# A Mamba-2 scan in front of expert routing: decays along rows of `a`, y's halves by sequences, states summed in PSUM

## Chip, cores and metric

One core of one Trainium2 chip runs the kernel. The metric is device time in microseconds (us). Times are medians over repeated executions; the profile is one execution of its own.

## What is computed

The first block is a Mamba-2 scan over 4 sequences b, 8 heads h, 768 positions, head width D = 32 and state width N = 16. The second sends each of the 3072 tokens (256 channels, all heads of one position) through one of 8 experts, chosen by a hash of its token id.

```python
log_a = np.log(np.clip(a, 1e-06, 1.0))
for c in range(nc):                                # chunks of positions
    cum = np.cumsum(la, axis=-1)
    L = np.exp(cum[:, :, :, None] - cum[:, :, None, :]) * causal
    y_intra = np.einsum('bhij,bhjd->bhid', np.einsum('bhin,bhjn->bhij', Cc, Bc) * L, xc)
    y_inter = np.einsum('bhin,bhnd->bhid', Cc, state) * np.exp(cum)[:, :, :, None]
    y[:, :, sl] = y_intra + y_inter
    decay_from_j = np.exp(cum[:, :, -1:] - cum)
    Bx = np.einsum('bhjn,bhjd->bhjnd', Bc, xc) * decay_from_j[:, :, :, None, None]
    state = np.exp(np.sum(la, axis=-1))[:, :, None, None] * state + np.sum(Bx, axis=2)
...
expert_idx = token_ids * np.int64(2654435761) % np.int64(E)
for e in range(E):
    xe = x[expert_idx == e]
    out[expert_idx == e] = np.maximum(xe @ w1[e], 0.0) @ w2[e]
```

## The kernel before

All orders are written by hand: each engine and each DMA queue runs its instructions in the order of the program, and waits only for data and for buffers.

The positions are cut into 6 pairs k of 128 positions, each pair into two units u of 64. Two pairs make a chunk ck of 256 positions (three chunks). The logarithms of `a` are summed inside a unit and turned into factors `fac` (exp of plus and minus the sum, measured from the middle of the unit) with which `scale_rows` multiplies the rows of C (i = 1) and B (i = 0). So a unit's masked product needs no L of its own.

For a chunk: `scale_rows` (DVE or POOL) writes `rows`. `squares` turns them on TensorE (PE) into PSUM, and `take_b` and `take_c` copy them out as `bt` and `ct`. `spread_c` writes four copies `ce` of `ct`, each with all but one head of four set to zero by `par4`. `steps_b` turns `bt` back into `ben` with the positions on the partitions.

For a pair: `gram` (32 matmuls of 64 x 64 by 256 columns, into PSUM banks 0 to 3) makes the products of C and B, and `masked` copies their causal part into `m_sb` on DVE, two instructions a pair. `dstates` (32 matmuls into bank MB = 6) makes what each unit adds to the state; ACT copies it to `d_sb`, and `states` then runs the recurrence on DVE: add (`zd`, L337), decay (`z`, L341), and a spread form `z4` (L344, DVE or POOL). `intra` (64 matmuls) and `inter` (32 matmuls of 64 x 128 columns) sum y in banks 4 and 5. There a PSUM half (64 partitions) holds four heads, and a bank holds two of the four sequences. `y_evict` copies y out on ACT (L383) and `y_store` sends it to `y_tokens` in HBM in runs of 512 bytes. `gram` and `dstates` run one pair ahead.

Between these stand the pieces of the routing: counts of tokens by expert (`rt_count`), then `piece(0)` to `piece(8)` on DVE, POOL and PE, which end in index lists. In `piece(4)` POOL makes 18 one-hot lists (`rt_lanes`, L541). After `y_store` of pair 3 POOL fetches 7 tiles of tokens by index (`gather`, L610), after that of pair 5 the rest. The experts' stage follows: `up` (L869) and `down` (L914) on PE with sums of weights on POOL and of activations on DVE, outputs scattered by POOL. Its weights are loaded by SP, most of them behind the first gather after pair 5 (`held`).

At the start `a` is loaded so that each partition holds 8 neighbouring positions of every head and chunk, in runs of 32 bytes. Sums over 8 are finished by two fp32 matmul pairs with selectors (`wsel`), before the exponentials; `decays_of_units` does the same for the decay of a unit with `usel`.

## Time and profile before

| | |
|---|---|
| median of 3 runs | 279.69 us (279.38 to 280.7) |
| profiled execution, time | 281.92 us |
| profiled execution, span from first to last instruction | 280.2 us |
| mean granted TensorE clock | 0.918 of full speed |
| first `gram` starts | 21.23 us |
| `y_evict` of pairs 0, 2, 5 starts | 31.58, 57.91, 85.74 us |
| first matmul of the experts' stage | 91.47 us |

Times inside the trace count from the start of the span. An engine's busy time says little here, since the stages have different limits; what is to be read is what the instruction that ended a stage had waited for.

### The profile page before, as it was taken

The page shows a single profiled execution, that of the slowest core. Times are in us where ns is not written, and L with a number is a line of the kernel's source. Part 1 is how long each engine was busy: PE and PEld are TensorE (multiplying, and loading weights), DVE is VectorE, ACT ScalarE, POOL GpSimd, SP SyncE. Part 2 cuts the span into 40 slices and gives each one's busy share as a digit, 9 for nine tenths or more (in the row PEclk, how much of TensorE's full clock was granted, in tenths as well). Part 3 has the DMA queues.
Part 4 walks back from the last instruction along what each step waited for, and adds up shares of the span by engine and source line. Part 5 has one row for each costly group of instructions (what it writes and reads, how often), then busy time and mean ns, then how long its engine had stood idle before and what let it go on. Part 6 is the DMA issues. An engine that isn't in the chain of part 4 may idle for free.

```text
span 280.2 us, 5428 instructions
## 1 busy us (share of the span) xinstructions
PE 236.3 (84%) x2066; PEld 214.3 (76%) x2066; DVE 198.0 (71%) x309; ACT 81.8 (29%) x168; POOL 187.5 (67%) x208
## 2 busy tenths in 40 slices
PE   6569886957994976957999899999999995999980
PEld 2355774745892966947999799999998995999870
DVE  4589999849280521696779978968689889577710
ACT  0536361260222551500221133232323322232110
POOL 8895169994036428998049979999699995192223
PEclk9676998695999797995999999999999999799998
DMA  7999577138269469440271731921511600410011
GB/s 116 167 177 151 116 124 135 17 80 147 42 158 276 152 174 357 148 165 2 64 256 47 234 133 45 292 96 40 168 37 45 203 23 19 150 37 22 20 37 56
DMA packets 55904, 33.12 MB, mean 118 GB/s; under 512 B 29708, under 2 KB 50212, under 8 KB 55878
## 3 DMA queue, kind: packets, MB, share of 16 engines
q1 hardware_dynamic: 50786, 25.74, 38.8%
q0 software_dynamic: 2400, 6.43, 6.9%
q10 hardware_dynamic: 2692, 0.60, 1.4%
q8 instruction: 17, 0.28, 0.5%
q14 instruction: 9, 0.07, 0.1%
HBM read 26.47 MB, written 6.42 MB: 117 GB/s over the span
## 4 chain that ended last, share of the span: by engine, by line
PE 48%; DVE 21%; DMA 19%; issue 5%; POOL 3%; ACT 2%; SPq 1%; POOLq 0%; DVEq 0%; ACTq 0%
PE ps L869 16%; PE ps L914 14%; DMA out_dram<-o_sb,idx_out 9%; DVE t L834 5%; PE ps L305 5%; DMA w<-in_moe_w_dram 4%; PE ps L362 4%; DVE ce L284 3%; PE ps L375 3%; DMA raw<-in_B_dram 2%; PE ps L254 2%; ACT y_sb L383 1%; DVE hx L896 1%; DMA y_tokens<-y_sb 1%; DMA xg<-y_tokens,idx_in 1%
## 5 line engine op out<-in xcount | busy, mean ns | idle before, releaser
L950 POOL DMA_INDIRECT out_dram<-o_sb,idx_out x25 | 29.6, 1182 | 34.8 <-ACT o_sb L946 27.1
L825 POOL TENSOR_TENSOR s<-w 128x512 f32<-128x512 f32 x30 | 39.4, 1312 | 15.2 <-DMA w<-in_moe_w_dram 14.8
L869 PE MATMUL ps<-t,s 128*128 128x202 f32 (+7 forms) x192 | 39.9, 344 | 5.4 <-DVE u L884 5.4
L610 POOL DMA_INDIRECT xg<-y_tokens,idx_in x25 | 28.0, 1119 | 23.4 <-DVE m L311 14.4
L869 PEld LDWEIGHTS ps<-t,s 128*128 128x128 f32 x192 | 34.1, 201 | 6.0 <-issue 5.7
L914 PE MATMUL ps<-t,s 128*128 128x202 f32 (+7 forms) x192 | 35.7, 329 | 0.2 <-DVE t L846 0.2
L914 PEld LDWEIGHTS ps<-t,s 128*128 128x128 f32 x192 | 32.4, 192 | 0.4 <-issue 0.4
L869 PE MATMUL ps<-xT,w 128*128 128x202 f32 (+7 forms) x128 | 26.5, 343 | 3.2 <-DMA w<-in_moe_w_dram 3.2
L869 PEld LDWEIGHTS ps<-xT,w 128*128 128x128 f32 x128 | 22.4, 201 | 3.5 <-issue 3.5
L834 DVE TENSOR_TENSOR t<-xT 128x202 f32<-128x202 f32 (+7 forms) x16 | 20.5, 1282 | 4.0 <-ACT xT L624 4.0
L305 PE MATMUL ps<-ce,bt 64*64 64x256 f32 x192 | 17.2, 510 | 5.2 <-DVE ce L284 5.2
L897 ACT ACTIVATE hx<-hx 128x404 f32<-128x404 f32 (+7 forms) x16 | 8.1, 524 | 44.8 <-DVE hx L896 44.8
L825 POOL TENSOR_TENSOR s<-s,w 128x512 f32<-128x512 f32 x15 | 19.8, 1322 | 0.7
L825 POOL TENSOR_TENSOR s<-w,s 128x512 f32<-128x512 f32 x15 | 20.0, 1335 | 0.2
L305 PEld LDWEIGHTS ps<-ce,bt 64*64 64x64 f32 x192 | 9.2, 177 | 10.5 <-issue 7.5
L884 DVE TENSOR_TENSOR u<-ps,p 128x404 f32<-128x404 f32 (+7 forms) x16 | 8.7, 556 | 11.1 <-PE ps L869 10.9
L914 PE MATMUL ps<-t,w 128*128 128x202 f32 (+7 forms) x64 | 12.7, 343 | 4.1 <-DVE du L931 4.0
L875 ACT ACTIVATE p<-ps 128x404 f32<-128x404 f32 (+7 forms) x16 | 7.9, 492 | 26.5 <-PE ps L869 26.2
L848 DVE SCALAR_TENSOR_TENSOR t<-hx 128x808 f32<-128x808 f32 (+7 forms) x8 | 15.2, 1894 | 0.0
L311 DVE COPY_PREDICATED m<-cmask,ps 128x1024 f32<-128x1024 int32 x12 | 15.0, 1300 | 0.0
L914 PEld LDWEIGHTS ps<-t,w 128*128 128x128 f32 x64 | 10.8, 195 | 5.2 <-DVE du L931 5.2
L337 DVE TENSOR_TENSOR zd<-d_sb,z 128x256 f32<-128x256 f32 x10 | 6.8, 680 | 11.2 <-ACT d_sb L327 11.1
(190 smaller groups left out, 510.3 us busy)
## 6 DMA issues: line engine op xcount, KB each, us to landing
w<-in_moe_w_dram SPq DMA_DIRECT2D x16, 512.0 KB, 5.6
w<-in_moe_w_dram SPq DMA_DIRECT2D x8, 1024.0 KB, 5.4
xb<-in_x_dram SPq DMA_DIRECT2D x12, 256.0 KB, 6.3
y_tokens<-y_sb SPq DMA_DIRECT2D x12, 256.0 KB, 4.5
raw<-in_B_dram SPq DMA_DIRECT2D x12, 128.0 KB, 4.0
raw<-in_C_dram SPq DMA_DIRECT2D x8, 128.0 KB, 4.1
raw<-in_C_dram ACTq DMA_DIRECT2D x4, 128.0 KB, 4.5
xg<-y_tokens,idx_in POOLq DMA_INDIRECT x25, 3.4
```

The costliest lines, as they stand in the source:

```text
L284: eng.tensor_scalar(out=o, in0=i, scalar1=par4[:, e:e + 1], scalar2=None, op0=OP.mult)
L305: pe.matmul(out=ps[u * T:(u + 1) * T, GB + 2 * m + h, i * HH * T:(i + 1) * HH * T].rearrange("q (e i) -> q e i", e=HH), lhsT=bts[ck][r, b, ...
L311: dve.copy_predicated(out=m_sb[k % 2][:, m].rearrange("q h b e i -> q h (b e i)"), mask=cmask.bitcast(I32).rearrange("q j i -> q (j i)").u ...
L362: pe.matmul(out=o[:, :, h4], lhsT=m_sb[k % 2][:, b // 2, h, b % 2, h4], rhs=xs[k][:, :, b, HH * h + h4], start=first(b // 2, h), stop=True ...
L610: pool_e.indirect_dma_start(out=xg[k], out_offset=None, in_=y_dram[0:n, :], in_offset=bass.IndirectOffsetOnAxis(ap=idx_in[:, k:k + 1], axi ...
L825: eng.tensor_tensor(out=s[:, i], in0=a_, in1=b_, op=o)
L834: dve.tensor_tensor(out=t[:, i], in0=a_, in1=b_, op=OP.subtract)
L848: dve.scalar_tensor_tensor(out=t[:, 2], in0=q(0, 1), scalar=0.0, in1=q(1, 1), op0=OP.max, op1=OP.subtract)
L869: pe.matmul(out=ps[:, bank, i * n:(i + 1) * n], lhsT=lhs[:, (q0 + i) * P:(q0 + i + 1) * P], rhs=rhs, start=(first and i == 0), stop=True, ...
L884: dve.tensor_tensor(out=st["u2"], in0=src, in1=st["p1"], op=OP.add)
L914: pe.matmul(out=ps[:, bank, 0:n], lhsT=lhs(q), rhs=rhs(q), start=(first and q == 0), stop=True, skip_group_check=True)
L950: st = pool_e.indirect_dma_start(out=out[:], out_offset=bass.IndirectOffsetOnAxis(ap=idx, axis=0), in_=o_sb, in_offset=None, bounds_check= ...
```

## The change

- **Decays.** `a` is loaded as 24 rows of 1 KB for each sequence (one row is one head's 256 positions of a chunk). DVE sums along the row, subtracts the value in the middle of each unit (`rel`), and turns blocks of 32 x 32 (`dve.transpose`), so that the exponentials read SBUF. `wsel` and `usel` go, with their POOL work; selectors are made from the identity by five reductions and a copy on DVE. Unit decays come from two products on POOL and two matmuls.
- **Order of loads.** C of chunk 0 moves from ACT's queue to SP's, in front of B's; the token ids go behind ACT's first table load; x of pair 1 goes ahead of the rows of chunk 1.
- **Squares halved.** `squares`, `take_b` and `take_c` become `square`: four transposes into one bank and one copy, all copies on ACT.
- **States in PSUM.** The ACT copy `d_sb` goes. DVE adds the old state onto the PSUM tile in place and multiplies from there; `z4` is made from `z` by two ACT instructions with a selector scale `pm`.
- **y's halves.** A PSUM half now holds two sequences and a bank four heads, so that `inter` takes its rows from either half of the partitions and writes either half: four quarters of the array in turn, where it was two. `y_store` writes runs of 1 KB.
- **Order.** `m_sb[0]` is cleared on DVE at the start; `x` of pair 0 partly by ACT. At pair 0 `gram(1)` goes ahead of `dstates(0)`, and `piece(0)` and `piece(1)` behind the state updates. The squares and `spread_c` of chunk 1 move from the end of pair 0 to pair 1, behind `piece(1)` to `piece(3)` on DVE. The spread of chunk 2 moves from behind the state updates of pair 3 into the middle of pair 2. In pairs 3 and 4 `intra` goes ahead of the next `gram`.

```diff
-    a_t = apre.tile([P, H, CK, RR], F32)
+    UC = CT // T
+    HCK = H * CK
+    a_row = apre.tile([P, CT], F32)
+    dve.memset(a_row, 1.0)
     for b in range(NB):
-        (sp_e, act)[b % 2].dma_start(out=a_t[32 * b:32 * b + 32],
-                                     in_=a[b].rearrange("h (c p r) -> p h c r", c=CK, r=RR))
+        (sp_e, act)[b % 2].dma_start(out=a_row[32 * b:32 * b + HCK], in_=a[b].rearrange("h (c x) -> (h c) x", x=CT))
...
+    load_rows(0, 1, sp_e)
...
+    load_rows(0, 0, sp_e)
+    load_x(0)
+    load_x(1)
+    load_rows(1, 1, sp_e)
+    load_rows(1, 0, sp_e)
+    load_x(2)
...
+    def selectors():
+        blocks = ident.rearrange("q (b m) -> q b m", b=NB)[:, :, 0:HCK]
+        dve.tensor_reduce(out=sbc, in_=blocks.rearrange("q b (h c) -> q b c h", c=CK), axis=AX.X, op=OP.add)
+        dve.tensor_reduce(out=hsel, in_=blocks.rearrange("q b (h c) -> q h b c", c=CK), axis=AX.XY, op=OP.add)
+        dve.tensor_copy(out=hsels, in_=hsel.unsqueeze(2).to_broadcast([P, H, NS]))
+        dve.tensor_reduce(out=par4, in_=ident.rearrange("q (b e n) -> q e b n", b=2, e=HH), axis=AX.XY, op=OP.add)
+        dve.tensor_reduce(out=par, in_=ident.rearrange("q (b e n) -> q e b n", b=NB, e=2), axis=AX.XY, op=OP.add)
+        dve.tensor_reduce(out=pm, in_=ident.rearrange("q (h g x) -> q g h x", h=2, g=2), axis=AX.XY, op=OP.add)
+
+    def decays_of_units(bank, eng):
+        s4 = [P, CK, UC, NB]
+        for i, v in enumerate((rel[:, :, T - 1], cum[:, :, T // 2 - 1])):
+            eng.tensor_tensor(out=ends[:, i], in0=v.unsqueeze(1).unsqueeze(3).to_broadcast(s4),
+                              in1=sbc.rearrange("q b c -> q c b").unsqueeze(2).to_broadcast(s4), op=OP.mult)
+        f = lambda i: ends[:, i].rearrange("q c v b -> q (c v b)")
+        l = hsels.rearrange("q h n -> q (h n)")
+        pe.matmul(out=ps[:, bank, 0:NU * NB], lhsT=l, rhs=f(0), start=True, stop=False, skip_group_check=True)
+        pe.matmul(out=ps[:, bank, 0:(NU - 1) * NB], lhsT=l, rhs=f(1)[:, NB:], start=False, stop=True,
+                  skip_group_check=True)
+        act.activation(g_sb.rearrange("q u b -> q (u b)"), ps[:, bank, 0:NU * NB], AF.Exp)
+        for e in range(2):
+            act.activation(gm[:, :, :, e], g_sb, AF.Copy, scale=par[:, e:e + 1])
 
...
+        dve.tensor_scalar(out=a_row, in0=a_row, scalar1=1e-6, scalar2=1.0, op0=OP.max, op1=OP.min)
+        act.activation(a_row, a_row, AF.Ln)
         act.activation(warm, rst[:, 0, 1:2], AF.Exp)
-
-    def decays_b():
-        f3 = lambda t: t.rearrange("q h c r -> q (h c) r")
-        f2 = lambda t: t.rearrange("q h c r -> q (h c r)")
-        dve.tensor_tensor_scan(out=f2(cum), data0=rst.rearrange("q k r -> q (k r)"), data1=f2(a_t), initial=0.0,
-                               op0=OP.mult, op1=OP.add)
-        dve.tensor_copy(out=cnt.rearrange("q i e c -> q (i e c)"), in_=ps[:, 6, 0:2 * E * NCH])
-        NA = HC * RR
-        pe.matmul(out=ps[:, 3, 0:NA], lhsT=ident, rhs=f2(cum), start=True, stop=False, skip_group_check=True)
-        pe.matmul(out=ps[:, 3, 0:NA].rearrange("q (k r) -> q k r", r=RR), lhsT=wsel[:, 0].rearrange("q u i -> q (u i)"),
-                  rhs=f3(cum)[:, :, RR - 1:RR].to_broadcast([P, HC, RR]), start=False, stop=True, skip_group_check=True)
-        for i in range(2):
-            act.activation(f2(fac[:, i]), ps[:, 3, 0:NA], AF.Exp, scale=(-1.0, 1.0)[i])
+        dve.tensor_tensor_scan(out=f(cum), data0=f(rst), data1=a_row, initial=0.0, op0=OP.mult, op1=OP.add)
+        dve.tensor_tensor(out=rel, in0=cum, in1=cum[:, :, T // 2 - 1:T // 2].to_broadcast([P, UC, T]), op=OP.subtract)
+        dve.transpose(out=relT, in_=f(rel).rearrange("q (p r) -> q r p", r=RR))
+        for i in (1, 0):
+            act.activation(fac[:, i], relT[:, :, 0:HCK], AF.Exp, scale=(-1.0, 1.0)[i])
 
...
+    def square(ck, i, h, bank, eng):
+        ts = (bts, cts)[i]
+        if ck not in ts:
+            ts[ck] = asq.tile([P, NB, CT], F32, name=("bt", "ct")[i], bufs=2)
+        for r in range(4):
+            pe.transpose(out=ps[:, bank, r * P:(r + 1) * P], in_=rows[ck, i][:, 4 * h + r], identity=ident)
+        o = ts[ck].rearrange("q b (p r) -> q b p r", r=RR)[:, :, :, 4 * h:4 * h + 4]
         if eng is act:
-            act.activation(o, sq(bank, h), AF.Copy)
+            act.activation(o, sq(bank), AF.Copy)
         else:
-            dve.tensor_copy(out=o, in_=sq(bank, h))
+            dve.tensor_copy(out=o, in_=sq(bank))
 
...
-        ds[k] = awork.tile([P, NB, 2, 2 * D], F32, name="d_sb", bufs=1)
-        act.activation(ds[k].rearrange("q b u f -> q (b u f)"), ps[:, MB], AF.Copy)
-
-    def states(k, eng):
-        for u in range(2):
+
+    def states(k, us=(0, 1)):
+        for u in us:
             un = 2 * k + u
             if un == NU - 1:
                 continue
-            t = ds[k][:, :, u]
+            t = ps[:, MB].rearrange("q (b u f) -> q b u f", b=NB, u=2)[:, :, u]
             if un > 0:
-                s = awork.tile([P, NB, 2 * D], F32, name="zd", bufs=3)
-                dve.tensor_tensor(out=s, in0=t, in1=zs[un].rearrange("q b e d -> q b (e d)"), op=OP.add)
-                t = s
-            if un + 1 < NU - 1:
-                z = zs[un + 1] = awork.tile([P, NB, 2, D], F32, name="z", bufs=2)
-                dve.tensor_tensor(out=z, in0=t.rearrange("q b (e d) -> q b e d", e=2),
-                                  in1=gm[:, un].unsqueeze(3).to_broadcast([P, NB, 2, D]), op=OP.mult)
-            z = z4s[un + 1] = awork.tile([P, NB, 2, 2, D], F32, name="z4", bufs=3)
-            eng.tensor_tensor(
-                out=z, in0=t.rearrange("q b (e d) -> q b e d", e=2).unsqueeze(2).to_broadcast([P, NB, 2, 2, D]),
-                in1=gm4[:, un].rearrange("q b (g e) -> q b g e", g=2).unsqueeze(4).to_broadcast([P, NB, 2, 2, D]),
-                op=OP.mult)
+                dve.tensor_tensor(out=t, in0=t, in1=zs[un].rearrange("q b e d -> q b (e d)"), op=OP.add)
+            z = zs[un + 1] = awork.tile([P, NB, 2, D], F32, name="z", bufs=3)
+            dve.tensor_tensor(out=z, in0=t.rearrange("q b (e d) -> q b e d", e=2),
+                              in1=gm[:, un].unsqueeze(3).to_broadcast([P, NB, 2, D]), op=OP.mult)
+            z4 = z4s[un + 1] = awork.tile([P, NB, 2, 2, D], F32, name="z4", bufs=3)
+            for g in range(2):
+                act.activation(z4[:, :, g].rearrange("q b e d -> q b (e d)"), z.rearrange("q b e d -> q b (e d)"), AF.Copy,
+                               scale=pm[:, g:g + 1])
 
...
+            for j in range(2):
                 for h in range(2):
-                    r = slice(64 * h, 64 * h + 64)
-                    c = ((b % 2) * 2 + u) * HH * D
-                    pe.matmul(out=ps[r, YB + b // 2, c:c + HH * D], lhsT=cts[ck][r, b, kk * P + u * T:kk * P + (u + 1) * T],
-                              rhs=z4s[2 * k + u][r, b].rearrange("q g e d -> q (g e d)"), start=first(b // 2, h),
-                              stop=True, skip_group_check=True)
+                    for v in range(2):
+                        b, r = 2 * v + j, slice(64 * h, 64 * h + 64)
+                        c = (j * 2 + u) * HH * D
+                        pe.matmul(out=ps[64 * v:64 * v + 64, YB + h, c:c + HH * D],
+                                  lhsT=cts[ck][r, b, kk * P + u * T:kk * P + (u + 1) * T],
+                                  rhs=z4s[2 * k + u][r, b].rearrange("q g e d -> q (g e d)"), start=first(h, v),
+                                  stop=True, skip_group_check=True)
 
...
+        o = y_dram[k * NB * P:(k + 1) * NB * P].rearrange("(v j i) s -> v i j s", v=2, i=T)
+        for v in range(2):
+            sp_e.dma_start(out=o[v], in_=t[64 * v:64 * v + 64].rearrange("q j u s -> q (j u) s"))
 
...
+    dve.memset(m_sb[0], 0.0)
+    clear_x(0, act, (0,))
+    selectors()
+    decays()
+    clear_x(0, act, (1,))
+    decays_of_units(7, pool_e)
+    filler(4, 3)
+    scale_rows(dve, 0, 1, 0, 4)
+    scale_rows(dve, 0, 1, 4, 8)
+    square(0, 1, 0, YB, act)
     rt_ids_a()
+    filler(1, 3)
+    square(0, 1, 1, YB + 1, act)
     rt_ids_b(6)
     rt_mask()
     rt_count(6)
+    scale_rows(dve, 0, 0, 0, 4)
     scale_rows(dve, 0, 0, 4, 8)
     for e in range(HH):
         spread_c(0, e, dve, 0)
+    square(0, 0, 0, GB, act)
+    filler(1, 3)
+    square(0, 0, 1, GB + 1, act)
...
+        if k == 0:
+            grams()
+            dstates(0)
+            states(0)
+            piece(0)
+            intra(0)
+            inter(0)
+            y_evict(0)
+        elif k == 1:
+            for i in range(2):
+                for h in range(2):
+                    square(ck + 1, 1 - i, h, GB + 2 * i + h, act)
+            for e in range(HH):
+                spread_c(ck + 1, e, (dve, act)[e % 2])
+            intra(k)
+            inter(k)
+            y_evict(k)
+            steps_b(ck + 1)
+            grams()
+        elif even and more:
+            square(ck + 1, 1, 0, BQ, act)
+            grams()
+            square(ck + 1, 1, 1, MB, act)
+            intra(k, (0,))
+            square(ck + 1, 0, 0, BQ, act)
+            for e in range(HH):
+                spread_c(ck + 1, e, (dve, act)[e % 2])
+            intra(k, (1,))
+            square(ck + 1, 0, 1, MB, act)
+            inter(k)
+            y_evict(k)
+        else:
+            if not even and nxt:
+                steps_b(ck + 1)
+            intra(k)
+            if nxt:
+                grams()
+            inter(k)
+            y_evict(k)
         y_store(k)
         if nxt:
             dstates(k + 1)
...
+            states(k + 1)
         if k == 0:
+            piece(1)
+            clear_x(2, pool_e)
             piece(2)
             piece(3)
```

## Rows read from the trace of the kernel before

**Rows 1.** Busy time by stretch: length, then each engine (instructions), granted clock, DMA.
```profile
41.10:57.90 16.80, 14.32 (x220) 10.58 (x220) 13.79 (x22) 3.67 (x4) 15.25 (x21) 0.80 0.38 64
...
91.50:280.20 188.70, 165.95 (x989) 161.60 (x988) 134.26 (x192) 50.94 (x123) 128.55 (x103) 0.95 0.34 112
...
64.00:68.00 4.00, 3.55 (x32) 1.98 (x32) 3.93 (x6) 0.00 (x0) 2.39 (x2) 0.50 1.11 189
```

**Rows 2.** The chain that ended last, 0 to 92 us: start, us, what.
```profile
15.68 5.51 DVE ce L284 x4
...
21.23 3.69 PE ps L305 x32
...
31.58 1.02 ACT y_sb L383
...
45.43 2.35 POOL rows L246 x2
...
57.91 1.02 ACT y_sb L383
...
62.84 1.48 DVE ce L284 x2
...
71.17 1.89 PE ps L375 x32
73.07 1.01 PE ps L322 x32
...
74.80 1.89 PE ps L305 x32
76.68 2.02 PE ps L362 x64
...
85.74 1.03 ACT y_sb L383
...
87.42 3.54 DMA y_tokens<-y_sb
```

**Rows 3.** Timeline, 0 to 25 us: start, us, engine, line, operation, count [idle before].
```profile
2.61 0.51 DVE L422 TENSOR_SCALAR eid_i<-tok 24x128 int32<-24x128 int32 x1 [0.69 <-DMA tok<-in_moe_token_ids_dram]
...
5.06 0.27 DVE L676 TENSOR_REDUCE par<-ident 128x4 f32<-128x128 f32 x1
...
6.05 0.53 DVE L223 TENSOR_SCALAR a_t<-a_t 128x192 f32<-128x192 f32 x1 [0.53 <-DMA a_t<-in_a_dram]
...
8.12 0.56 DVE L230 TENSOR_TENSOR_SCAN cum<-rst,a_t 128x192 f32<-128x192 f32 x1 [1.54 <-ACT a_t L224]
...
10.86 3.04 DVE L246 TENSOR_TENSOR rows<-raw,fac 128x512 f32<-128x512 f32 x3 [1.74 <-ACT fac L238]
...
12.70 1.80 POOL L701 MEMSET m<- 128x2048 f32 x1
...
18.45 1.34 PE L289 MATMUL ps<-ident,bt 128*128 128x128 f32 x8 [1.22 <-ACT bt L263]
...
21.10 2.37 DVE L445 TENSOR_TENSOR_SCAN pin<-rstc,cnt 128x192 f32<-128x192 f32 x1
...
22.10 2.54 ACT L282 ACTIVATE ce<-ct,par 128x512 f32<-128x512 f32 x4
```

**Rows 4.** Timeline, 38 to 67 us, same columns.
```profile
38.20 0.57 DVE L476 TENSOR_TENSOR shift<-sel,pin 128x8 f32<-128x8 f32 x1
...
42.97 0.21 DVE L472 CAST place_i<-whof 128x8 int32<-128x8 f32 x1
...
45.49 1.32 DVE L337 TENSOR_TENSOR zd<-d_sb,z 128x256 f32<-128x256 f32 x1
...
52.79 13.59 POOL L541 TENSOR_SCALAR laneoh<-iota,lane 128x128 bf16<-128x128 f32 x18 [0.35 <-DVE stile L530]
...
59.61 0.42 DVE L337 TENSOR_TENSOR zd<-d_sb,z 128x256 f32<-128x256 f32 x1 [4.42 <-ACT d_sb L327]
```

**Rows 5.** The page, costliest groups: busy us, mean ns of one, idle before.
```profile
L884 DVE TENSOR_TENSOR u<-ps,p 128x404 f32<-128x404 f32 (+7 forms) x16 | 8.7, 556 | 11.1 <-PE ps L869 10.9
```

More of the change, by code (lines that the diff above doesn't have):

```diff
@@ L314, in masked @@
             data=ps[:, GB + 2 * m:GB + 2 * m + 2])
-    ds, zs, z4s = {}, {}, {}
+    zs, z4s = {}, {}
     def dstates(k):
@@ L354, in first, with intra @@
         return f
[L356 to L364 removed]
+    def intra(k, hs=(0, 1)):
+        for h in hs:
+            for j in range(2):
+                for h4 in range(HH):
+                    for v in range(2):
+                        b = 2 * v + j
+                        o = ps[64 * v:64 * v + 64, YB + h, j * 2 * HH * D:(j + 1) * 2 * HH * D].rearrange("q (u f) -> q u f", u=2)
+                        pe.matmul(out=o[:, :, h4 * D:(h4 + 1) * D],
+                                  lhsT=m_sb[k % 2][:, v, h, j, h4], rhs=xs[k][:, :, b, HH * h + h4],
+                                  start=first(h, v), stop=True, skip_group_check=True)
     def inter(k):
@@ L706 @@
     masked(0, 1)
-    for e in range(2):
-        act.activation(gm[:, :, :, e], g_sb, AF.Copy, scale=par[:, e:e + 1])
-    for e in range(HH):
-        act.activation(gm4[:, :, :, e], g_sb, AF.Copy, scale=par4[:, e:e + 1])
-    for e in range(HH):
-        spread_c(0, e, act, 1)
-    dstates(0)
-    consts_late()
+    act.activation(cnt.rearrange("q i e c -> q (i e c)"), ps[:, 6, 0:2 * E * NCH], AF.Copy)
+    steps_b(0, MB)
+    pool_e.memset(m_sb[1], 0.0)
     clear_x(1, pool_e)
@@ L732, with grams @@
         begun.clear()
-        if even and more and not late:
-            squares(ck + 1, 1, bank=MB)
-            take_c(ck + 1, act)
-        if not even and nxt:
-            steps_b(ck + 1)
-        if nxt and k != 1:
+        def grams():
             for m in range(2):
@@ L741 @@
                 masked(k + 1, m)
-        if even and more and not late:
-            squares(ck + 1, 0, bank=MB)
-            take_b(ck + 1, MB)
-        intra(k)
-        inter(k)
-        y_evict(k)
+        if k == 0:
[29 more added lines that the diff above has]
+            y_evict(k)
+        else:
+            if not even and nxt:
[5 more added lines that the diff above has]
+            y_evict(k)
         y_store(k)
-        if nxt and k == 1:
-            for m in range(2):
-                gram(k + 1, (m,))
-                masked(k + 1, m)
         if nxt:
             dstates(k + 1)
-        if late:
-            squares(ck + 1, 1, bank=MB)
-            take_c(ck + 1, act)
-            squares(ck + 1, 0, bank=GB)
-            take_b(ck + 1, GB)
-        if nxt:
-            states(k + 1, pool_e if k < 2 else dve)
-        if even and more:
-            for e in range(HH):
-                spread_c(ck + 1, e, (dve, act)[e % 2])
+            states(k + 1)
         if k == 0:
+            piece(1)
+            clear_x(2, pool_e)
             piece(2)
```

147 lines of the change are left out of this document (37 added, 110 removed).

## Prediction, written before the change was run

> **What bounds the kernel now.** I read the busy time by stretch first [rows 1]. From 91.5 us to the end the experts' stage runs 188.7 us with PE busy for 166 of them. The change touches nothing in it. Before that lies the scan, where no engine is full: from 41.1 to 57.9 us DVE is busy 13.8 of 16.8 and PE 14.3 at a granted clock of 0.80. So the scan is bound by its chains of waits.
>
> The chain that ended last [rows 2] then names the waits, with `y_evict` as milestones: pair 0 at 31.58, pair 2 at 57.91, pair 5 at 85.74. [...] Four spreads on DVE take 5.51 us (15.68 to 21.19) while POOL is at work, and the first `gram` waits for them. POOL's `rows` at 45.43 hold the squares of chunk 2 back. Two spreads of twice the size at 62.84 take only 1.48. [...] Last come the stores of y (3.54 us for the one in the chain), and the experts' stage starts behind them.
>
> The timelines [rows 3, 4] give the durations, the page the price of a DVE operation on PSUM [rows 5].
>
> **To the first `gram`: 21.23 becomes 16.8.** Before, the clamp of `a` waited for its load until 6.05, and the scan at 8.12 for ACT, whose queue first issued the loads of C. After the scan came two matmul pairs and the exponentials, and `rows` began at 10.86, 2.2 us behind the scan's end [rows 3]. `a` now arrives in 96 runs in place of 3,072, and I take it as landed before DVE wants it. DVE's first clears end at 1.92 (idle 0.69 before 2.61). It then clears the new `a_row` (256 columns, 0.2 by the 1.80 of 2048) and `m_sb[0]` (1.80, moved from POOL), and runs five reductions and a copy (0.27 each at most, 1.6): 5.5. The clamp has 256 columns for 192 (0.7), Ln 0.5 (my value), the scan 0.75 by the same ratio: 7.45. Subtraction and block transpose are not shown alone. From below stands 0.35 each (an operation on 404 columns takes 0.556 [rows 5]), from above 1.32 (256 columns while POOL reads too [rows 4]); POOL has lost the work on `wsel` and `usel`, so I take 0.4 each: 8.25. One exponential, 0.35: `rows` of C begin at 8.6. Two of them (3.04 / 3 each) end at 10.6. The token ids, once done in the wait for `a`, are now in line: four instructions of 0.51 or less, and a transpose on PE between, 1.8. The two `rows` of B end at 14.4. Four spreads: before 1.38 each, but half of 0.74 to 0.74 by the undisturbed pair of 1024 columns. POOL now has its clears behind it and waits for rows of chunk 1, so 0.5 each, 16.4. `bt` is ready at about the same time (four cold transposes 0.67, a copy 0.64 behind 14.4). With 0.4 for waits between engines: 16.8, a gain of 4.4. If POOL meets the spreads, 3.5 of it is lost.
>
> **Pair 0: 31.58 becomes 28.0.** The same matmuls take the same 10.35 us, and `steps_b(0)`, which had run under the spreads (1.34 at 18.45 [rows 3]), now stands behind the first `gram`; the shorter `inter` gives back 0.5. Gain left: 3.6.
>
> **`inter`.** 32 matmuls of 128 columns on two quarters take 1.89. `gram` goes round all four quarters already, and takes the same 1.89 for 32 of 256 columns [rows 2]. Half of that is 0.95. From above, nothing is gained; from below stands half of the 2.02 that 64 matmuls of `intra` take, about 1.0, which shows how fast short ones can follow each other. I take 1.0, a gain of 0.9 a pair.
>
> **States.** The ACT copy leaves the chain from `dstates` to the states. An add or multiply on PSUM with one SBUF operand is 0.35 by proportion (0.556 for 404 columns [rows 5]); I take 0.4, four a pair. Its upper end is 1.32, which `zd` took beside POOL with both operands in SBUF [rows 4]. `z4` is two ACT instructions of 256 columns, 0.32 to 0.64 (2.54 / 4 for 512 [rows 3]); I take 0.42, 1.7 a pair, on an engine that had been busy 3.7 of 16.8 us. The price is that bank 6 stays taken while DVE works: 1.6 us in which the next transposes there cannot start.
>
> [...]
>
> **Pair 1: `gram(2)` starts at 38.7 where it was 41.1.** This is where most of the lead goes. DVE now has the spreads of chunk 1 behind the pieces. States of pair 0 are ready at 27.0; `piece(0)` (a scan of up to 2.37 [rows 3] and small ones) 2.7, states of pair 1 1.6, `piece(1)` 0.9, `piece(2)` and `piece(3)` 5.0 (38.20 to 43.18, 20 instructions [rows 4]), two spreads 1.5: 38.7. PE will by then have idled some 3 us, so I take this `gram` at 3.69: it ends at 42.4 against 43.0.
>
> **Pair 2: 57.91 becomes 50.6.** `dstates(2)` 1.0. POOL's `rows` of chunk 2 were started some 6 us earlier and no longer hold anything. PE needs 7.3 (four squares at 0.33, `gram` 1.9, `intra` 2.0, `inter` 1.0, `dstates` 1.0). ACT needs more: `z4` to 45.3, three copies to 47.3, two spreads (1.27 each), a copy: 50.6, then `y_evict`. Gain 7.3.
>
> **Pairs 3 to 5: 27.8 us become 19.3.** Pair 3: `dstates` 1.0, states 1.6 with PE waiting for bank 6, `steps_b` 1.1, `intra` 2.0, `gram` 1.9, `inter` 1.0, in sum 8.6. Pair 4: `dstates` 1.0, the table 0.7, and 4.9 for the other three, 6.6. Pair 5 4.1. The spreads that stood in front of the slow `gram` at 64 are long done. That would put the last `y_evict` at 69.9, a gain of 15.8.
>
> **What I take off.** POOL's 18 lists take 13.59 [rows 4] from about 47.2 (states of pair 2, then `piece(4)`'s small ones), so the table waits until 60.8 and PE with it: 1.0. One more `gram` or `intra` at the lower clock: 1.5. I count nothing for the longer runs of `y_store` (at most 1 of 3.54).
>
> **Sum.** 4.4 - 0.8 - 3.0 + 6.7 + 8.5 - 2.5 = 13.3 us. The profiled execution took 281.92 (span 280.2), 2.2 above the median of the runs; I carry the difference over, so 268.6 for such an execution and **266.4** for the median.
>
> **Rivals.**
> - *Four quarters run no faster than two.* `inter` stays at 1.89 and 5 us are lost: 271.4. For it: these matmuls have half of `gram`'s columns, so loading weights may show. Against it: `intra`'s 64 short ones follow at 0.032. Chance 0.10.
> - *The lists come late, or POOL still holds DVE* (the change not doing what it says for the states). If states and pieces run at the 1.32 of [rows 4] in pairs 1 and 2, `piece(4)` starts 5 to 7 us later, and the 13.59 us of lists, the table and the first gathers move with it: 272.4. For it: the lead in pair 1 is 2.4 and DVE has no gap there. Against it: one SBUF operand in place of two. Chance 0.16.
> - *Slower: the clock.* If PE's new gaps keep it at the lower level through the scan, `gram` costs 1.8 more in four pairs, `intra` 1.0 in six, `inter`, `dstates`, `steps_b` and squares together some 6: 13.8 or more on top of what I have taken off, with the slow start of pair 0 about 17 in all: 283. It decides from about 13 us of lost clock. For it: 0.50 from 64 to 68 behind a PE gap [rows 1]. Against it: the whole of 41.1 to 57.9 had 0.80 with gaps of its own. Chance 0.06.
> - *More than the forecast*, below 260, if pair 1 is shorter and no `gram` is cold: 0.05. *No change within 0.5%* (about what these runs can tell): 0.03.
>
> **Numbers.** The forecast has 0.60 and spans 260 to 270.5 (spreads 3.5, subtraction and transpose 1.8, clock 1.8 either way). With the first two rivals up to 274, the range 260 to 274 holds about 0.8. Faster by over 0.5%: 0.60 + 0.10 + 0.16 + 0.05 = 0.91; the same 0.03; slower 0.06.
>
> **What would show it.** In the profile after: the first `gram` near 16.8; four spreads in some 2 us; 32 `inter` matmuls in about 1.0; `gram(2)` near 38.7, with PE idle before it and DVE busy; state operations near 0.4 also while POOL works; `y_evict` of pairs 2 and 5 near 51 and 72; the experts' stage as long as before. The prediction is wrong if `a` or the rows of C land after 8.6, if DVE's pieces stretch beyond 38.7, if PE waits for the lists beyond 62, or if the experts' stage gains or loses on its own.

## The result, and the profile after the change

The changed kernel takes 266.06 us, the median of four runs (264.19 to 267.9), and the kernel before 280.19 in the runs beside it: a ratio of 0.9505, with a 95% interval of 0.941 to 0.96. The forecast was 266.4. The profiled execution took 266.91 (span 265.2) where 268.6 was forecast for one. A ratio compares the fast runs of the two kernels alone, so it need not be the quotient of the medians.

The chain that ended last, of the changed kernel (start, us, what):

```profile
12.90 1.29 DVE rows L245 x2
14.19 1.60 DVE ce L274 x4
...
15.92 1.96 PE ps L295 x32
...
33.82 1.99 DVE ce L274 x2
...
35.95 3.34 PE ps L295 x32
...
51.36 1.09 PE ps L279 x8
52.45 3.56 PE ps L347 x64
56.02 1.89 PE ps L295 x32
57.91 0.87 PE ps L361 x32
...
67.03 1.74 PE ps L347 x53
68.77 8.38 issue
77.15 1.02 ACT y_sb L370
```

Against [rows 2], the four spreads on DVE take 1.60 where they took 5.51, the first `gram` (L295) starts at 15.92 instead of 21.23 and takes 1.96 instead of 3.69, and an `inter` (L361) is a piece of 0.87 instead of 1.89. But one piece has no counterpart: "issue" for 8.38 us ahead of the last `y_evict`, which starts at 77.15. An engine in "issue" waits for nothing that the profile shows. The timeline of the changed kernel (start, us, engine, line, operation [idle before it, and what ended it]) shows what PE did in that time:

```profile
22.48 0.42 DVE L326 TENSOR_TENSOR z<-ps,gm 128x256 f32<-128x256 f32 x1
22.94 0.43 DVE L324 TENSOR_TENSOR ps<-ps,z 128x256 f32<-128x256 f32 x1
...
24.68 1.00 ACT L370 ACTIVATE y_sb<-ps 128x1024 f32<-128x1024 f32 x1
...
48.11 1.02 ACT L370 ACTIVATE y_sb<-ps 128x1024 f32<-128x1024 f32 x1
...
65.35 1.02 ACT L370 ACTIVATE y_sb<-ps 128x1024 f32<-128x1024 f32 x1 [2.51 <-PE ps L361]
...
66.81 1.25 POOL L597 DMA_INDIRECT xg<-y_tokens,idx_in  x1 [10.44 <-issue]
...
69.04 0.44 PE L361 MATMUL ps<-z,ct 64*64 64x128 f32 x7
69.67 0.43 PE L361 MATMUL ps<-z,ct 64*64 64x128 f32 x3 [0.19 <-issue]
70.38 0.46 PE L361 MATMUL ps<-z,ct 64*64 64x128 f32 x5 [0.27 <-issue]
...
74.90 1.00 POOL L597 DMA_INDIRECT xg<-y_tokens,idx_in  x1 [0.31 <-issue]
...
78.72 4.39 PE L863 MATMUL ps<-xT,w 128*128 128x202 f32 x12 [1.36 <-ACT xT L625]
```

The `inter` of pair 5 starts at 69.04 and would be over in 1.1 us, as the ones before it. After seven matmuls it goes on in handfuls of two to five, most of them about 0.73 us apart, until 74.6; the early transposes behind it come one to five at a time until 77.35. POOL's seven early gathers run from 66.81 to 75.9. The experts' first matmul starts at 78.72.

Busy time by stretch of the changed kernel (length, then PE, PEld, DVE, ACT, POOL with their instructions, granted clock, DMA share, GB/s):

```profile
17.00:28.00 11.00, 10.94 (x232) 8.54 (x224) 10.07 (x16) 4.42 (x9) 7.00 (x6) 1.00 1.15 170
28.00:39.00 11.00, 6.83 (x130) 5.22 (x124) 8.18 (x28) 7.17 (x12) 7.09 (x12) 0.84 0.95 201
...
51.00:60.00 9.00, 8.64 (x179) 7.51 (x180) 5.69 (x8) 3.28 (x5) 5.37 (x8) 0.81 0.85 166
...
69.00:77.15 8.15, 5.43 (x42) 3.13 (x40) 0.00 (x0) 0.00 (x0) 5.37 (x6) 0.74 0.68 207
77.15:265.20 188.05, 166.10 (x989) 161.50 (x988) 134.25 (x192) 52.55 (x125) 129.33 (x103) 0.94 0.35 114
```

From 17 to 28 us PE is busy nearly throughout; from 28 to 39 it is not (6.83 of 11), so there the scan is still bound by its waits, as in [rows 1]. From 69 to 77.15 it does 42 matmuls in 8 us, with DVE and ACT idle. From the last `y_evict` to the end it is 188.05 us; before, it was 280.2 - 85.74 = 194.46 [rows 1, 2].

So two things stood in the result that nobody had forecast: a stall of about 7 us in pair 5, and 6.4 us less behind it. The experiments ask what they are, and which parts of the change carry the gain.

### The profile page after: what moved, and what is told of

Read it like the earlier page. It is cut to its first block, busy times and chain, and to the rows that moved or that the text cites. A ratio compares the mean times of both kernels' runs of the same rounds, so it can differ in the third digit from the quotient of the medians.

```text
span 265.2 us, 5401 instructions
## 1 busy us (share of the span) xinstructions
PE 226.3 (85%) x2055; PEld 206.3 (78%) x2055; DVE 187.6 (71%) x311; ACT 89.3 (34%) x187; POOL 173.8 (66%) x191
## 4 chain that ended last, share of the span: by engine, by line
PE 43%; DVE 26%; DMA 16%; issue 9%; ACT 2%; POOL 1%; SPq 0%; DVEq 0%; POOLq 0%; ACTq 0%
PE ps L863 15%; PE ps L908 15%; DMA out_dram<-o_sb,idx_out 10%; DMA w<-in_moe_w_dram 6%; DVE t L828 5%; PE ps L295 4%; PE ps L347 2%; DVE m L301 2%; DVE hx L890 2%; DVE ce L274 1%; PE ps L935 1%; DVE t L840 1%; PE ps L312 1%; PE ps L259 1%; DVE z L326 1%
## 5 line engine op out<-in xcount | busy, mean ns | idle before, releaser
L819 POOL TENSOR_TENSOR s<-w 128x512 f32<-128x512 f32 x30 | 40.0, 1334 | 13.9 <-DMA w<-in_moe_w_dram 13.5
L597 POOL DMA_INDIRECT xg<-y_tokens,idx_in x25 | 28.7, 1149 | 22.6 <-issue 14.9
L863 PE MATMUL ps<-xT,w 128*128 128x202 f32 (+7 forms) x128 | 27.1, 348 | 3.8 <-DMA w<-in_moe_w_dram 2.4
L828 DVE TENSOR_TENSOR t<-xT 128x202 f32<-128x202 f32 (+7 forms) x16 | 18.7, 1168 | 2.1 <-ACT xT L611 2.1
L819 POOL TENSOR_TENSOR s<-w,s 128x512 f32<-128x512 f32 x15 | 19.3, 1286 | 0.2
L295 PE MATMUL ps<-ce,bt 64*64 64x256 f32 x192 | 13.2, 417 | 4.4 <-DVE ce L274 4.4
L842 DVE SCALAR_TENSOR_TENSOR t<-hx 128x808 f32<-128x808 f32 (+7 forms) x8 | 16.2, 2031 | 0.0
L330 ACT ACTIVATE z<-z,pm 128x256 f32<-128x256 f32 x22 | 10.0, 502 | 15.1 <-DVE z L326 14.8
L347 PE MATMUL ps<-xb,m 128*64 128x64 f32 x384 | 14.6, 239 | 0.4 <-DVE m L301 0.3
L347 PEld LDWEIGHTS ps<-xb,m 128*64 128x64 f32 x384 | 13.5, 152 | 1.7 <-issue 0.7
```

The costliest lines, as they stand in the source:

```text
L295: pe.matmul(out=ps[u * T:(u + 1) * T, GB + 2 * m + h, i * HH * T:(i + 1) * HH * T].rearrange("q (e i) -> q e i", e=HH), lhsT=bts[ck][r, b, ...
L330: act.activation(z4[:, :, g].rearrange("q b e d -> q b (e d)"), z.rearrange("q b e d -> q b (e d)"), AF.Copy, scale=pm[:, g:g + 1])
L347: pe.matmul(out=o[:, :, h4 * D:(h4 + 1) * D], lhsT=m_sb[k % 2][:, v, h, j, h4], rhs=xs[k][:, :, b, HH * h + h4], start=first(h, v), stop=T ...
L597: pool_e.indirect_dma_start(out=xg[k], out_offset=None, in_=y_dram[0:n, :], in_offset=bass.IndirectOffsetOnAxis(ap=idx_in[:, k:k + 1], axi ...
L819: eng.tensor_tensor(out=s[:, i], in0=a_, in1=b_, op=o)
L828: dve.tensor_tensor(out=t[:, i], in0=a_, in1=b_, op=OP.subtract)
```

## The experiments

They were made in four sittings, each on a chip of its own, with runs of the kernel before beside it: 284.2 us in the first, 280.9 in the second, 276.5 in the third, 281.6 in the fourth. Ratios are to those runs; total times are compared within a sitting only.

**1. The weights' loads moved away from the stall.** Theory A of the first sitting: the loads of the experts' weights, issued between the last pairs, starve PE.

```
-        if k >= 2 and k < 5:
-            load_w1(k - 2, 0)
+        if k == 2:
+            load_w1(0, 0)
+            load_w1(1, 0)
+        if k == 3:
+            load_w1(2, 0)
```

> The changed kernel with one move: the first half of w1 of experts 1 and 2 is loaded one pair earlier, so that no weights are under way while PE works on pair 5. Theory A (PE's instructions come over the DMA rings and were held up behind the weights from 69 to 77 us): the last inter runs through in about 1.1 us, the last y_evict starts at 70 to 71 in place of 77.15, and the time falls by 3 to 7 us to about 260. Theory B (that stretch of PE's program is starved whatever the weights do): the gaps of about 0.7 us for five matmuls stay, the last y_evict stays near 77, the time stays at 266 within 1.

269.51 us, ratio 0.9595 (0.9485 to 0.9705). The last load of weights ahead of pair 5 is now issued at 63.51, and the stall stays. It now begins in `intra` of pair 5, at 70.2, and the last `y_evict` is at 81.03. Theory A falls.

**2. PE's program shifted.** 32 tiny matmuls at the start put everything on PE 64 instructions later in its program.

```
     decays()
+    for _ in range(32):
+        pe.matmul(out=ps[:, 7, 0:8], lhsT=fill16[:, 0:P], rhs=fill16[:, 0:8], start=True, stop=True)
     clear_x(0, act, (1,))
```

> The changed kernel with 32 matmuls of 8 columns put into PE's idle time at 4 to 8 us, so that all later PE instructions lie 64 places further on in the program; the work is otherwise the same. If the starved stretch belongs to a place in PE's program (blocks of instructions), it begins 32 matmuls earlier, in intra of pair 5 near 68 us; if it belongs to the moment and its traffic, it stays in the last inter near 69; if it belongs to inter on four quarters, it stays in inter. Time within 1 us of the changed kernel under the first two.

273.74 us; its runs gave no ratio. The stall begins at 71.1 in `intra` of pair 5, and the last `y_evict` is at 81.27. A stall bound to a place in the program would have moved 64 instructions back in it, out of `inter` and into `intra`, and so it did; but run 1 moved it into `intra` with the program's places kept. What runs 1 and 2 share with the first profile is the time: 2.6 to 3.3 us after POOL's first early gather (66.81, 66.94, 68.51). That became theory C: the stall follows the gathers.

**3. `inter` with the row halves outside.**

```
-            for j in range(2):
-                for h in range(2):
+            for h in range(2):
+                for j in range(2):
                     for v in range(2):
```

> The changed kernel with the loops of inter the other way round, so that only two quarters of the array follow each other (same matmuls, same layout). Theory of the forecast: 32 matmuls go back from about 1.08 to about 1.9 us, and 5.5 pairs lose 4 to 5 us: last inter begins near 73 and the time is 269 to 271, unless the later arrival at pair 5 removes the starved stretch, which would give part of it back (266). Rival, four quarters gain nothing: unchanged.

271.34 us, ratio 0.9645 (0.948 to 0.9809). The median is near the 269 to 271 that was expected of a slow `inter`, but the rows have none: in pairs 1 to 4 the 32 matmuls take 1.10 to 1.15 us all the same, and the profiled execution took 264.48. The loop over the row halves stands inside that over `u`, so the halves still change after every four matmuls: the run did not bring `inter` down to two quarters, and does not answer its question. Run 9 does.

**4. The states' copy in SBUF restored.** ACT copies `dstates` into `d_sb` again, and the adds read that. To make room, `bt` has one buffer instead of two (not shown here).

```
+        ds[k] = awork.tile([P, NB, 2, 2 * D], F32, name="d_sb", bufs=1)
+        act.activation(ds[k].rearrange("q b u f -> q (b u f)"), ps[:, MB], AF.Copy)
...
-            t = ps[:, MB].rearrange("q (b u f) -> q b u f", b=NB, u=2)[:, :, u]
+            t = ds[k][:, :, u]
```

> The changed kernel with ACT's copy of the state increments to SBUF put back and the recurrence run there (bt in one buffer, to make room). Theory of the forecast: the copy costs 0.6 us of ACT a pair and lengthens the chain from dstates to the states, DVE's adds (two SBUF operands) grow from 0.43 to up to 1.2 where POOL works on tensors, but bank 6 comes free 1.2 us earlier in pair 3: in sum 0 to 4 us slower. Rival: nothing of it is on the path, the time stays within 1 us.

265.86 us, ratio 0.9452 (0.9373 to 0.9532). That is no slower than the change: summing in PSUM, priced in the forecast at some gain, bought nothing that these runs can tell. Its timeline, at the transposes into bank 6 and the `intra` of pair 3:

```profile
51.70 1.09 PE L279 MATMUL ps<-ident,bt 128*128 128x128 f32 x8 [0.72 <-ACT d_sb L317]
52.73 2.08 PE L349 MATMUL ps<-xb,m 128*64 128x64 f32 x64
```

With the copy PE waits 0.72 us for bank 6, where the change has 2.01 (until 51.36), and the `intra` behind the wait takes 2.08, where it took 3.56 in the result's chain, at a granted clock of 0.53. The `y_evict` of pair 4 is at 64.14 with the copy and at 65.35 without.

**5. The changed kernel again**, as the yardstick of the second sitting.

> The changed kernel once more, as the yardstick of the three runs beside it. All theories: the time within 1% of 266.1 us, and the stall there again: matmuls of pair 5 in dribbles with PE waiting for nothing that the profile shows, beginning 2 to 5 us after POOL's first early gather and over 1 to 3 us after its seventh, with the last y_evict near 77 us.

268.83 us, ratio 0.9464 (0.9383 to 0.9546). The stall is there: gathers from 67.48, stall from 70.7, last `y_evict` at 81.22. But this execution was 3 us late long before that. Its timeline:

```profile
17.41 3.61 PE L295 MATMUL ps<-ce,bt 64*64 64x256 f32 x32 [0.69 <-ACT bt L262]
...
27.81 1.00 ACT L370 ACTIVATE y_sb<-ps 128x1024 f32<-128x1024 f32 x1
```

The first `gram` takes 3.61 where it took 1.96, and the first `y_evict` is at 27.81 instead of 24.68. Over the ten profiles with the change's prologue untouched (that of the result and nine here) this goes two ways: 1.96 in four, 3.45 to 3.69 in six. The forecast had counted the first `gram` at 3.69.

**6. All early gathers held until the last `y_evict`**, by a copy of one column of `y_sb` on POOL ahead of them.

```
-        if k == 3:
-            for q in EK:
-                gather(q, early=True)
+        if k == 5:
+            pool_e.tensor_copy(out=held1, in_=ysb[k][:, 0, 0, 0:1])
+            for q in EK[0:]:
+                gather(q, early=True)
```

> POOL's seven early gathers wait for the last y_evict (a copy of one column of y_sb on POOL ahead of them); the loads of the experts' weights stay where they are. Theory C (the seven gathers crowd PE's instructions out of the transfers): intra and inter of pair 5 run through, inter in 1.1 us, and the last y_evict starts at 69.5 to 71 us instead of 77. What follows then starts with gathers that are some 5 us later than before, so the time moves by less: 263 to 270 us. Rival P (the stall belongs to the place in PE's program, or to the weights' loads, and comes whatever POOL does): the stall is in pair 5 still, the last y_evict stays at 76 to 78 us, and the time grows by 3 to 7 us because the gathers only begin then.

267.48 us, ratio 0.9512 (0.945 to 0.9574). Its timeline:

```profile
67.82 1.02 ACT L370 ACTIVATE y_sb<-ps 128x1024 f32<-128x1024 f32 x1 [2.51 <-PE ps L361]
...
71.50 1.10 PE L361 MATMUL ps<-z,ct 64*64 64x128 f32 x32
...
72.72 1.02 ACT L370 ACTIVATE y_sb<-ps 128x1024 f32<-128x1024 f32 x1 [1.50 <-issue]
...
81.59 1.97 PE L617 MATMUL ps<-ident,xg 128*128 128x128 f32 x8 [8.98 <-DMA xg<-y_tokens,idx_in]
...
83.39 1.04 PE L865 MATMUL ps<-xT,w 128*128 128x202 f32 x2
```

The stall is gone: `inter` of pair 5 runs through in 1.10, and the last `y_evict` comes 4.9 us after that of pair 4 (13.2 in run 5). Yet the time is that of run 5, because PE now waits 8.98 us for the first gathered rows; the experts start 10.7 us behind the last `y_evict`, where they had started 1.6 behind it. In this run what the missing stall gives is lost again to the wait; runs 9 and 10 will show that the one does not need the other.

**7. Three early gathers in their place, four held.** The edit is run 6's with `EK[:3]` left at `k == 3` and `EK[3:]` held.

> Three of the seven early gathers go where they went, the other four wait for the last y_evict. Theory C: the stall is there but shorter, about three sevenths (3 us of 7), the last y_evict at 72 to 74 us. A variant of C, in which the queues only fill up after some gathers: no stall, 70 us. Rival P: 76 to 78 us, as with all seven.

269.7 us, ratio 0.957 (0.951 to 0.963). The idle time that PE spends in "issue" in pair 5 shrinks to 0.26 and 0.38 us, in `intra` ahead of 70.17 and 70.91, and the last `y_evict` comes 5.8 us after that of pair 4. That is less than three sevenths of the stall, so it is not proportional to the gathers, and nearer to the variant that expected none. The fourth gather is now late: PE waits 6.56 us for its rows, until 81.60.

**8. Spreads of chunk 1 between the router's pieces 2 and 3.**

```
         if k == 0:
             piece(1)
             clear_x(2, pool_e)
+            for i in range(2):
+                for h in range(2):
+                    square(ck + 1, 1 - i, h, GB + 2 * i + h, act)
             piece(2)
+            for e in range(HH):
+                spread_c(ck + 1, e, (dve, act)[e % 2])
             piece(3)
```

(with the same lines taken out of `k == 1`).

> In pair 1 the transposes and evictions of chunk 1 go ahead of the router's pieces 2 and 3 in the program, and the six spreads between the two pieces, where they stood behind both. If gram(2) waits for DVE's order alone (pieces 2 and 3 take 4.5 us ahead of the spreads), it starts 2 us earlier than 36.0 and the y_evicts of pairs 1 to 4 move with it by 1 to 2 us; the router's lists then end up to 2 us later, which costs nothing while the table's matmuls come at 60. Rival: the stall of pair 5 takes the gain, and the last y_evict stays within 1 us of where it is; time within 0.5%.

266.87 us, ratio 0.9459 (0.938 to 0.9537), the same as run 5. Its timeline:

```profile
35.80 1.96 PE L295 MATMUL ps<-ce,bt 64*64 64x256 f32 x32 [0.98 <-ACT ce L272]
...
40.73 0.66 PE L259 MATMUL ps<-ident,rows 128*128 128x128 f32 x4 [1.96 <-POOL rows L245]
41.32 3.58 PE L295 MATMUL ps<-ce,bt 64*64 64x256 f32 x32
...
50.24 1.02 ACT L370 ACTIVATE y_sb<-ps 128x1024 f32<-128x1024 f32 x1
```

`gram(2)` starts 2.5 us earlier than in run 5 (38.28), takes 1.96 instead of 3.42, and so is done 4 us earlier. The next `gram` gives it back: the transposes ahead of it wait 1.96 us for POOL's rows of chunk 2, which stand behind piece 3 on POOL, and then it is itself the slow one, 3.58. The `y_evict` of pair 2 has gained 0.3 us (50.52 in run 5).

**9. `inter` by row halves**, 16 matmuls on one, then 16 on the other: the loop over `h` outside that over `u`.

> inter's 32 matmuls go by row half: 16 with rows 0 to 63, then 16 with rows 64 to 127, with the column halves in turns, so that only two quarters of the array are in use at a time (nothing is left out). If the halving of inter comes of four quarters in turns: 1.7 to 1.9 us for the 32, as before the change. If two quarters with different columns do as well: 1.05 to 1.15 us.

One execution, 260.85 us, no ratio. The 32 take 1.54 to 1.59 us in its timeline (1.05 to 1.10 with the change, 1.96 before). So neither expectation was right: two quarters with different columns are faster than the two of the kernel before, and four are faster still. In stretches of four matmuls on a row half the 32 took 1.10 to 1.15 us (run 3), in stretches of sixteen 1.54 to 1.59.

**10. Idle matmuls in the gaps of the prologue.**

```
     clear_x(0, act, (1,))
+    filler(9, 3)
     decays_of_units(7, pool_e)
-    filler(4, 3)
+    filler(5, 3)
...
     rt_mask()
+    filler(3, 3)
     rt_count(6)
+    filler(1, 3)
...
+    filler(3, 3)
     gram(0, (0,))
```

(and `filler(2, 3)` for the first `filler(1, 3)`).

> Idle matmuls are added in the prologue's gaps on PE (nine ahead of the sums of units, one more behind them, five more up to the first gram, one of four left as it is), so that PE has work from 1.5 us to the first gram. Theory F (the executions of the changed kernel differ by the clock that the prologue gets: the first half of gram 1.96 us in some profiles and 3.4 to 3.7 us in others, the first y_evict at 24.7 or at 27 to 28): gram(0) takes 1.96 us, the first y_evict starts at 24 to 25.5 us, and the median falls by 0.5 to 1% against the changed kernel's (0.941 to 0.946 of before) with less spread. Rival: the clock falls here all the same, wherever the idle matmuls stand, gram(0) takes 3.4 us or more, or the added matmuls delay the transposes; the first y_evict is at 27 to 29 us and the ratio 0.95 to 0.96.

260.22 us, ratio 0.9351 (0.9238 to 0.9464). Its timeline:

```profile
1.53 5.94 PE L154 MATMUL ps<-fill 128*128 128x512 bf16 x15 [1.53 <-DVE fill L136]
...
15.67 1.96 PE L295 MATMUL ps<-ce,bt 64*64 64x256 f32 x32 [0.33 <-DVE ce L274]
...
24.41 1.00 ACT L370 ACTIVATE y_sb<-ps 128x1024 f32<-128x1024 f32 x1
...
64.87 1.25 POOL L597 DMA_INDIRECT xg<-y_tokens,idx_in  x1 [7.36 <-DVE idx_out L567]
...
68.62 1.10 PE L361 MATMUL ps<-z,ct 64*64 64x128 f32 x32
...
69.84 1.02 ACT L370 ACTIVATE y_sb<-ps 128x1024 f32<-128x1024 f32 x1 [1.50 <-issue]
...
72.93 1.00 POOL L597 DMA_INDIRECT xg<-y_tokens,idx_in  x1 [0.30 <-issue]
```

The first `gram` takes 1.96 and the first `y_evict` is at 24.41, as expected, at a granted clock of 1.00 from 6.7 us, where the record begins, to 34; run 12, with the same idle matmuls, has 1.96 and 24.43. These are two executions of two, and four of ten had 1.96 without the idle matmuls, so that the two are their doing is likely but not shown. That the time is better than the change's is likely but not shown, since the intervals meet. The expected narrower spread did not come: 256.81 to 269.32.

The lower rows hold a surprise. All seven gathers run from 64.87 to 73.9, and pair 5 runs through beside them: no stall. Runs 9 (seven gathers) and 11 (four), on the same chip, have none either. Nor has the kernel before. Its timeline, at pair 5:

```profile
80.82 1.26 POOL L610 DMA_INDIRECT xg<-y_tokens,idx_in  x1 [14.44 <-DVE m L311]
...
81.72 2.09 PE L362 MATMUL ps<-xb,m 128*64 128x64 f32 x64
...
83.73 1.96 PE L375 MATMUL ps<-z,ct 64*64 64x128 f32 x32
```

Its early gathers, too, begin right behind the `y_evict` of pair 4, four of the seven have started when `inter` of pair 5 ends at 85.7, and PE runs through until then, 4.9 us behind the first. So without gathers beside pair 5 the stall is gone (run 6), but gathers beside it are not enough to bring it about. What else it takes is open: the changed kernel itself was not run on the chip of runs 9 to 11, so whether the chip decides is not shown either.

**11. Four early gathers in their place, three held.**

> As the run with three early gathers in their old place, with four there and three behind the last y_evict, so that the first two early transposes have their rows. Theory C: the stall of pair 5 is short (1 to 2 us), the last y_evict at 72 to 75 us, the experts' first matmul 1.6 us after it, and the time 1 to 3 us under the changed kernel's: ratio 0.935 to 0.945. Rival (what the stall takes is hidden by the wait for the last pair's stores, the late gathers and the second experts' weights, which end last either way): the last y_evict comes early all the same, and the ratio stays at 0.945 to 0.957.

263.69 us, ratio 0.9442 (0.9311 to 0.9574). The last `y_evict` is at 68.42, but the experts' first matmul comes 5.0 us behind it, at 73.39, held up by the gathered rows, and PE then waits twice more for DVE (1.27 and 1.68 us). From the last `y_evict` to the end it is 191.7 us (187.5 in run 10 on the same chip). Neither expectation was right in full: the ratio is at the border of both ranges and there is no stall at all, but what came early is lost behind the last `y_evict`, as the rival had it, though to the gathered rows.

**12. The parts joined:** the idle matmuls of run 10, the spreads of run 8, and POOL's scaling of chunk 2's rows moved ahead of piece 3.

```
+            for i in range(2):
+                scale_rows(pool_e, 2, 1 - i, 0, 4)
+                scale_rows(pool_e, 2, 1 - i, 4, 8)
             piece(3)
-            for i in range(2):
-                scale_rows(pool_e, 2, 1 - i, 0, 4)
-                scale_rows(pool_e, 2, 1 - i, 4, 8)
```

> The idle matmuls of the prologue, the transposes and evictions of chunk 1 ahead of the router's pieces 2 and 3 with the six spreads between them, and POOL's scaling of chunk 2's rows ahead of piece 3 (which kept the second gram of pair 3 waiting when the spreads alone were moved); all seven early gathers where the change has them. If the gains add: gram(2) at 33 to 34 us and at the high clock, the y_evict of pair 2 at 45.5 to 47.5 us, that of pair 4 at 61 to 63.5, ratio to before 0.925 to 0.938 where pair 5 runs through and 0.93 to 0.945 where it stalls. Rival (DVE's order takes the middle's gain back, as when the spreads alone were moved): pair 2 at 48 to 50 us, ratio no better than the idle matmuls alone, 0.935 to 0.946.

265.93 us, ratio 0.9374 (0.9299 to 0.9448). The profiled execution was the longest of seven, 274.01. The rival was right: the `y_evict` of pair 2 is at 49.68, no earlier than with the idle matmuls alone (49.26), and pair 5 stalls again (78.44). Its timeline, beside two rows of the changed kernel's:

```profile
31.16 4.22 POOL L245 TENSOR_TENSOR rows<-raw,fac 128x512 f32<-128x512 f32 x4
31.26 1.01 DVE L468 TENSOR_SCALAR ov_i<-ov 128x8 int32<-128x8 f32 x1
32.31 1.02 DVE L469 TENSOR_SCALAR ov_i<-ov_i 128x8 int32<-128x8 int32 x1
...
36.87 3.69 PE L295 MATMUL ps<-ce,bt 64*64 64x256 f32 x32 [3.31 <-DVE ovt L477]
```

```profile
30.20 0.17 DVE L468 TENSOR_SCALAR ov_i<-ov 128x8 int32<-128x8 f32 x1
30.40 0.17 DVE L469 TENSOR_SCALAR ov_i<-ov_i 128x8 int32<-128x8 int32 x1
```

The reader is to see the same two instructions on eight columns: 0.17 us each with POOL idle, 1.01 beside POOL's `rows`, of which four take 4.22, so about one `rows` apiece. Four of them in a row cost 3.4 us ahead of the spreads, and `gram(2)` came at 36.87 where 33 to 34 was expected. Moving POOL's work forward put it over DVE's critical stretch.

In the result's trace the states' operations on PSUM with one SBUF operand take 0.42 to 0.43 us beside POOL's `rows` (those at 22.94 and 23.40) and beside its lists (49.49 to 50.88), as they do with POOL idle (59.93 to 61.32).

## Why the prediction was right, and where it was not

The total was right to 1.7 us on the profiled span (266.9 forecast, 265.2 measured), though two of its steps missed by over 6 us each, in opposite directions. By milestones, from the forecast's own numbers:

| Step | forecast | measured | difference |
|---|---|---|---|
| first `gram` starts | 16.8 | 15.92 | -0.9 |
| from there to `y_evict` of pair 0 | 11.2 | 8.76 | -2.4 |
| from there to `y_evict` of pair 2 | 22.6 | 23.43 | +0.8 |
| pairs 3 and 4 (15.2 and 2.5 taken off) | 17.7 | 17.24 | -0.5 |
| pair 5 | 4.1 | 11.80 | +7.7 |
| last `y_evict` to the end | 194.5 | 188.05 | -6.4 |

- **First `gram`: right, a little too careful.** Spreads were given 0.5 each and take 0.40 (1.60 for four); the block transpose and the subtraction, given 0.4 each, take 0.64 and 0.42; the clamp took 0.28 where 0.7 was allowed.
- **Pair 0: mis-sized by the clock.** The forecast kept the 3.69 of the slow `gram`. The profiled execution had 1.96, at a granted clock of 1.00 from 17 to 28 us (0.50 from 21 to 25 in the kernel before), but six of ten profiles had 3.45 to 3.69, so the forecast's value stands for most of them.
- **`inter`: right.** 1.0 was forecast; 0.87 in the chain (1.89 before) and 1.05 to 1.10 in the timeline (1.96 before) were measured. The rival with 1.89 falls.
- **States: the size was right (0.4 forecast, 0.42 and 0.43 measured), the worth was not.** Run 4 takes the step back and loses nothing: with the copy, too, all but one of their operations (1.30) take 0.42 to 0.55 us, where the forecast's upper end was 1.32, so POOL costs them little in this order either way. What ACT's copy cost, DVE's hold on bank 6 cost again: PE waits 2.01 us there, forecast at 1.6, and 0.72 with the copy.
- **`gram(2)`: right in kind.** It starts at 35.95 for 38.7, behind DVE's pieces and spreads, with PE idle 3.44 us, and is slow (3.34, at a granted clock of 0.59 from 35.9 to 39.4), as forecast. Run 8 showed that taking this wait away moves it on: the next `gram` waits for POOL and is slow in its place.
- **Taken off.** The lists end at 56.4, ahead of the table at 59.7, so the 1.0 for them was not needed. One more slow stretch did come, `intra` of pair 3 with 3.56 at a granted clock of 0.53 (from 52.4 to 56 us; 0.81 from 51 to 60): 1.5, as counted.
- **Pair 5: the step that failed.** The forecast had PE run through at 4.1, and it took 11.80. Its sum has no term for the early gathers beside `intra` and `inter`; the rows of the kernel before gave no reason for one, since there PE ran through beside them. Runs 6 and 7 show that the stall comes with the gathers; runs 1 and 2 that neither the weights' loads nor the place in the program make it. Why it comes here and not before, nor in runs 9 to 11, stays open, and so does what it is on PE's side: the profile shows no wait.
- **The experts' stage: the other step that failed.** "As long as before" took the stretch from the last `y_evict` as rigid, and it was 6.4 shorter. The experts' first matmul comes 1.57 us behind the last `y_evict`, where it came 5.7 behind it before (91.47 and 85.74), since the early rows lie ready by then. That is 4.2 us, but it is not shown to be a part of the 6.4: in runs 9 and 10 the seventh gather ends 5.1 and 4.1 us behind the last `y_evict` (4.2 before) and the first matmul comes 6.6 and 4.6 behind it, and the stretch to the end is 185.4 and 187.5 all the same. The first matmul is not on the changed kernel's chain; the weights that are loaded behind a late gather (`held`) are on it. Their pieces in the chain (start, us, what), in the kernel before, in the changed one and in run 10:

```profile
100.47 6.84 DMA w<-in_moe_w_dram
```

```profile
88.79 5.87 DMA w<-in_moe_w_dram
```

```profile
83.69 5.58 DMA w<-in_moe_w_dram
```

They land 21.6, 17.5 and 19.4 us behind the last `y_evict`, with 172.9, 170.5 and 168.0 us to go. So part of the 6.4 lies ahead of that landing and part behind it, and which part is the change's doing was not tried. The kernel before is known from one profile, of an execution 2.2 us above its median. Of the ten profiles with all seven gathers early, eight have 185.4 to 188.1 us from the last `y_evict` to the end (the executions of runs 2 and 12, over 274 us, have 191.9 and 193.9); with gathers held (runs 6, 7 and 11) it is 191.7 to 195.1.

That the two failures cancel, 7.7 against 6.4, is luck as far as these runs show. Run 6 gives the stall back (pair 5 in 4.9 us) and loses as much to the wait for gathers, but runs 9 and 10 have pair 5 in 4.9 us and the short stage at once. The total was right; it does not confirm these two steps. The rivals with the lists and with the clock fell for the changed kernel; POOL holding DVE, as the former has it, was seen in run 12 (1.01 us for 0.17 beside POOL's `rows`), where the order put it in the way.

No version here beats the change beyond doubt. The idle matmuls have the best ratio, 0.9351 (0.9238 to 0.9464), and their two profiles have the fast first `gram`; the joined version has 0.9374 (0.9299 to 0.9448).

## What to carry to other kernels

Check a forecast that came out right step by step: here a stall of 7 us and a stage that was 6.4 us shorter hid each other in the sum. Before a new stall is put down to what runs beside it, look whether the same ran beside it before; here the gathers did, and nothing stalled. Do not take the stage behind the change as rigid, even where nothing in it is edited. A wait taken away in the middle is worth nothing until the next one on the other engines is known, and moving POOL's work forward can cost DVE a full POOL instruction for each small one (run 12: four of them at 1.01 to 1.02 us, 0.17 with POOL idle).
